# Float64 weight bits: upper word scaled as float32 on ScalarE, two VectorE operations instead of three, and a new order of all engines

## The chip, the cores and the metric

One NeuronCore of a Trainium2 chip runs the whole kernel. The metric is the time of one execution on the device in microseconds (us); less is better. TensorE does the matmuls, VectorE, ScalarE and GpSimd (DVE, ACT and POOL in the profile) work on tiles in SBUF, and SyncE (SP) issues nearly all transfers.

## The reference

Retention, a linear attention with decay, feeds a gated MLP. Batch 4, 8 heads, 768 positions, head size 64, model width 512; all inputs float32 except the MLP's weights w_in and w_out, which come as float64.

```python
for t in range(S):
    state = gamma * state + outer(k[t], v[t])
    y[t] = scale * (q[t] @ state)
x = heads side by side in y
h = gelu_tanh(x @ w_in)
u, v = h[:512], h[512:]
v_n = (v - mean(v)) / sqrt(var(v) + 1e-6) * g_ln
v_s = w_sg @ v_n (over positions) + b_sg
out = x + (u * v_s) @ w_out
```

## The kernel before, in words

The work is cut into 4 batches (b) and 2 halves of 384 positions (hf). In a half, retention handles 4 pairs of heads (p), each in 6 chunks of 64 positions: scores sc and states ds by matmul into PSUM, a mask and a scan over chunk states on VectorE, then the output po, which VectorE multiplies by a growth factor into x (line 326). For the MLP every operand is split into a rounded part and its remainder (hi and lo), and each product is three matmul passes. The products are pv and pu (the two halves of w_in), ps (positions mixed by w_sg) and py (w_out). pv, pu, ps and py share four PSUM tiles, and ds, sc and po share four others.

The order of the work is written out by hand: PROG (lines 43 to 105) is a list of words, and every engine and every DMA queue does its own part in the order of the words. A word is a step's letter, then its place. L loads a pair, P scales its keys, S, D and O are the matmuls of sc, ds and po, T is the scan, M the mask, W and K copies of the states, X makes x, H and I its hi and lo; the digits are b, hf, p, so S101 is the scores of batch 1, half 0, pair 1 (and X013 the x of batch 0, half 1, pair 3). V and U are pv and pu; G and Y are ps and py; v and u are their gelus, s the statistics of a v tile, N the reciprocal root of the variances (12 small instructions that depend on each other, lines 375 to 382), n the normalisation, a and b hi and lo of v (tile vh); e, m, h, j make the gated tile gt and its hi and lo; r and y finish the output. A last letter D, G or A names VectorE, GpSimd or ScalarE where there is a choice. ~ puts warm-up matmuls (wp) on TensorE.

Weights have words of two letters and a number. Pieces v, u and o (four each, 128 x 512 float64, 512 KB, from w_in and w_out) and s (12 of 128 x 384 float32, 192 KB, from w_sg) are loaded by l. A float64 piece is then turned into a float32 with bit operations: k (ScalarE, line 175) takes the absolute value of the upper word read as a float32, b (VectorE) does three operations on it (lines 183, 184, 187) that move the exponent and mantissa into float32's places and add the sign, r (ScalarE, line 196) rounds the lower word, a (GpSimd, line 202) adds it. h and o then make hi and lo (line 223). A pair's load (L) is one kt of 384 KB and two mw of 192 KB, all on SyncE's queue with the weights, in the order of the words.

Of the kernel before, what the change touches and what calls it, by code (L numbers as in the profile page):

```python
# [48 lines left out]
lu1 T002 H010A D003 I010G M003 W0020A U0000 W0021A bu3 V0001 P012A V0021 X011 K002 au3 V0011 C012 T003 H011A
P013A S012 W0030A I011D O002 W0031G M012 hu3A D012 ro3 K003 S013 X002 L100 C013 ou3D H002A O003 ku1 T012 I002G  # L50
D013 ru1 ls9 M013 W0120G W0121A V0012 ls5 ls11 X003 V0002 L101 bu1 H003A V0022 O012 I003D lo2 T013 au1 P100A
lo0 U0001 hs9A ls4 X012 W0131A hs0G V0023 ls1 ls6 hu1A V0013 os9D v002 V0003 ou1D ls8 v001 s002 os0G U0100
u000 ls3 v000 s001 hs5G U0010 H012A ls2 s000 P101A W0130A I012D U0020 lo1 N00 os5G ro2 U0030 ro0 ls7 n000
U0011 ko0 n001 a000 n002 U0031 bo0 a001 ko2 U0021 hs3A bo2 hs11A O013 u003 hs1A os3D D100 hs10A X013 b000G
u002 D101 H013A T100 S100 hs4A b001G hs2A S101 u001 M100 L102 ko1 K100 V0120 ko3 ao2 M101 V0110 L103 ro1 V0121
hs8A I013D a002 os1D V0111 Q hs6A os10D V0122 hs7A b002D W1001A U0101 os7D os4D P102A V0123 bo1 u010 V0112
v012 os8D V0100 W1000A s012 os2G V0113 T101 P103A V0101 ao1 v011 U0110 W1011A s011 K101 ho1A ao0 V0102 W1010A
U0120 os11D os6D V0103 bo3 U0130 v010 s010 ho0G U0121 N01 U0131 oo1G u012 U0111 u013 n011 n012 O100 u011 n010
ao3 D102 a010 X100 a011 O101 T102 H100A b010G D103 a012 ho2A S102 b012D S103 b011D L110 I100D G0020 M103 ho3G
L111 G0000 X101 C110 oo0G M102 C111 G0021 oo3D G0001 H101G G0022 P110A oo2D G0002 I101G V1020 K102 e000 W1021G  # L60
G0010 P111A m000D V1021 W1020G h000 G0011 j000D T103 r000G V1000 G0012 W1031A K103 W1030G V1001 e001 e002 O102
m001G D110 X102 m002G h001 O103 T110 D111 H102G h002 S110 W1100A j001D S111 W1101G M110 L112 G0030 M111 j002G
C113 L113 G0110 T111 I102G C112 G0031 W1110A r001D X103 r002G W1111A V1022 V1002 H103G G0032 P112G G0111 e003
I103D Y0000 m003G P113A V1023 h003 r003G V1003 v102 j003G G0112 s102 v100 s100 Y0001 G0100 y000 G0120 G0101
G0121 G0102 G0122 e010 e011 U1000 m010D m011D Y0010 r010D r011G U1001 G0130 u100 Y0020 Y0011 Y0021 y001 V1010
y002 G0131 Y0030 G0132 h010 h011 j010D Y0031 j011G e012 V1011 m012G y003 Y0110 e013 h012 r012G Y0130 j012D
Y0100 m013G V1012 h013 r013G O110 j013D D112 X110 O111 H110G T112 D113 S112 W1120A I110D S113 X111 W1121A L200
M112 H111A Y0111 I111G M113 L201 Y0131 y011 T113 Y0101 y013 W1131G Y0120 y010 W1130G V1013 Y0121 P200G v101
s101 U1010 y012 N10 U1020 P201A U1030 n102 n100 U1021 n101 a100 U1100 a101 b100D u102 b101D a102 U1031 b102D
V1120 u103 U1011 V1121 u101 V1100 V1110 V1101 V1111 O112 D200 X112 O113 H112A T200 D201 I112G S200 K200 X113  # L70
S201 W2001G M200 L202 H113A V1122 I113G M201 V1102 L203 W2000G V1123 V1103 T201 v112 V1112 v110 s112 K201
U1110 W2010A s110 W2011A U1120 P202A V1113 U1121 v111 s111 P203A U1111 u112 N11 U1130 u111 U1101 n110 n112
a110 U1131 n111 u110 b110G a111 a112 O200 u113 b111D D202 X200 b112G O201 T202 D203 H200G W2020A S202 W2021A
S203 K202 M202 L210 I200G G1020 T203 C210 L211 G1100 X201 C211 K203 W2031A M203 G1021 H201A W2030A I201D G1101
G1022 P210G G1000 G1102 P211A G1010 G1001 G1011 G1002 G1012 e100 m100D G1030 e101 h100 r100G G1130 j100D m101D
G1031 e102 h101 r101G G1131 m102D j101D h102 G1032 r102G G1132 e103 j102D Y1000 m103G e110 Y1010 m110G h103
Y1020 r103D j103G O202 r110G D210 X202 O203 H202A T210 D211 I202G S210 W2101A W2100G S211 X203 L212 M210 H203A
Y1001 C213 I203G T211 C212 L213 Y1011 M211 W2110G Y1021 y100 W2111G y101 V2020 y102 G1120 P212A V2021 V2000
V2022 V2001 P213G V2023 V2002 v202 G1121 s202 U2000 V2003 U2001 v200 s200 U2010 u200 V2010 U2011 V2011 u201
G1122 V2012 G1110 V2013 G1111 v201 s201 Y1030 N20 G1112 h110 j110G Y1031 e111 n202 U2020 e112 m111D O210 m112D  # L80
h111 n201 h112 D212 y103 j111G O211 X210 T212 H210A D213 I210G S212 e113 W2121A S213 j112D L300 W2120A M212
m113G Y1120 T213 L301 h113 Y1110 M213 W2131A W2130G Y1130 X211 j113D U2021 H211A r111D n200 Y1121 u202 I211G
P300A Y1131 a200 r112D a201 r113G y112 Y1111 a202 b200D P301A U2030 y113 b201G y111 V2120 b202G V2100 U2031
V2101 u203 V2110 V2121 V2111 Y1100 O212 D300 X212 O213 H212G T300 D301 W3001A K300 S300 I212D S301 W3000G X213
L302 M300 H213A V2122 M301 Y1101 L303 T301 V2112 I213D V2102 W3011A y110 W3010G V2113 V2123 K301 v211 V2103
P302A s211 v212 U2100 v210 s212 U2110 s210 P303A N21 U2120 U2130 n210 n211 U2111 a210 n212 a211 b210G U2131
a212 u211 U2121 b212G u213 U2101 u212 b211G G2010 u210 G2030 G2000 G2031 G2001 G2032 G2020 G2002 G2021 e200
m200G G2100 r200D h200 G2022 j200D G2101 G2011 G2102 G2012 O300 e201 e202 D302 m201G X300 O301 H300A T302
# [496 lines left out]
```

## Time and profile before

| | |
|---|---|
| median of 3 runs | 412.82 us (412.26 to 413.41) |
| profiled execution | 414.86 us, its span 413.1 us |
| busy: TensorE | 400.7 us (97%) |
| busy: VectorE, GpSimd, ScalarE | 247.1, 155.2, 146.6 us |
| chain that ended last | TensorE 78%, VectorE 9%, DMA 9% |

Read first what TensorE does by stretch of time, then, where it waits, on whom. The busy time of matmuls is modelled from their starts, so the distance from one start to the next says more than the duration of one. A duration of a VectorE instruction includes what it waited for a port while running.

### The profile page before, as it was taken

How to read it: one execution, taken by the hardware profiler on the slowest of the kernel's cores; microseconds unless marked ns; L12 is line 12 of the kernel's file. 1: busy time of each engine (PE TensorE's matmuls, PEld its weight loads, DVE VectorE, ACT ScalarE, POOL GpSimd, SP SyncE). 2: the span in 40 equal slices, each digit the busy share in tenths (PEclk: the TensorE clock that was granted, in tenths of full speed). 3: DMA queues.
4: the chain of work that ended last, by engine and by line, in shares of the span. 5: the costliest groups of instructions: out<-in, count | busy, mean ns of one | idle time of the engine just before them, and what ended most of it. 6: DMA issues, size and time to landing. Idle time of an engine off the chain costs nothing.

```text
span 413.1 us, 9386 instructions
## 1 busy us (share of the span) xinstructions
PE 400.7 (97%) x3937; PEld 366.1 (89%) x3940; DVE 247.1 (60%) x488; ACT 146.6 (35%) x266; POOL 155.2 (38%) x161
## 2 busy tenths in 40 slices
PE   8998997999999999999999899999999999999996
PEld 3657886989999998999999898899998999899996
DVE  2799899987632674672761492741746855262652
ACT  4597687623411223442121152430234312230010
POOL 3446533638721530341651154230544133302421
PEclk9999999999999999999999999999999999999999
DMA  7999785032501070514042042500243210000012
GB/s 236 289 311 251 247 299 190 6 90 66 155 19 40 21 229 1 155 27 129 2 129 82 2 141 89 152 22 2 73 141 102 72 59 21 2 0 2 0 58 96
DMA packets 18123, 41.39 MB, mean 100 GB/s; under 512 B 2464, under 2 KB 8096, under 8 KB 18080
## 3 DMA queue, kind: packets, MB, share of 16 engines
q1 hardware_dynamic: 17936, 40.51, 32.6%
q8 instruction: 31, 0.51, 0.5%
q10 hardware_dynamic: 144, 0.27, 0.2%
q14 instruction: 12, 0.10, 0.1%
HBM read 34.48 MB, written 6.29 MB: 99 GB/s over the span
## 4 chain that ended last, share of the span: by engine, by line
PE 78%; DVE 9%; DMA 9%; issue 1%; ACT 1%; SPq 0%; ACTq 0%
PE ps L424 24%; PE py L462 16%; PE pv L351 13%; PE pu L407 13%; PE po L319 5%; DMA mw<-in_qv_dram 5%; PE sc L278 4%; PE ds L270 4%; DMA raw<-in_w_v_dram 2%; DMA tab<-in_c_tab_dram 1%; DMA raw<-in_w_sg_dram 1%; DVE ws L223 1%; DVE st L365 1%; DVE wx L187 1%; DVE mw L296 1%
## 5 line engine op out<-in xcount | busy, mean ns | idle before, releaser
L424 PE MATMUL ps<-ws,vh 128*128 128x384 f32 x576 | 105.7, 336 | 0.0
L424 PEld LDWEIGHTS ps<-ws,vh 128*128 128x128 f32 x576 | 100.6, 188 | 1.6
L407 PE MATMUL pu<-xh,wu 128*128 128x384 f32 x384 | 73.0, 339 | 1.6 <-DVE gt L434 1.1
L351 PE MATMUL pv<-wv,xh 128*128 128x512 f32 x288 | 74.1, 396 | 0.0
L462 PE MATMUL py<-gh,wo 128*128 128x384 f32 x384 | 72.1, 336 | 0.0
L407 PEld LDWEIGHTS pu<-xh,wu 128*128 128x128 f32 x384 | 67.5, 188 | 3.8 <-DVE gt L434 1.4
L462 PEld LDWEIGHTS py<-gh,wo 128*128 128x128 f32 x384 | 67.0, 188 | 0.7
L351 PEld LDWEIGHTS pv<-wv,xh 128*128 128x128 f32 x288 | 53.2, 188 | 9.5
L148 ACT COPY mw<-sq 64x320 f32<-64x320 f32 (+1 forms) x44 | 36.2, 822 | 29.9 <-DVE sq L283 29.6
L434 DVE SCALAR_TENSOR_TENSOR gt<-ps,gb 128x384 f32<-128x384 f32 x32 | 19.3, 612 | 43.8 <-PE ps L424 43.7
L449 ACT CAST gh<-gt 128x384 fp32r<-128x384 f32 x32 | 16.4, 514 | 74.5 <-POOL gt L445 31.3
L296 DVE TENSOR_TENSOR mw<-sc,tab 64x384 f32<-64x384 f32 x64 | 35.5, 555 | 9.4 <-PE sc L278 7.9
L365 DVE BATCH_NORM_STATS2 st<-v 128x6 f32<-128x512 f32 x24 | 16.4, 683 | 31.4 <-ACT v L361 31.4
L473 POOL TENSOR_TENSOR o<-xh 128x384 f32<-128x384 f32 x16 | 18.0, 1125 | 40.6 <-DVE gt L445 40.3
L326 DVE TENSOR_TENSOR x<-po,tab 128x384 f32<-128x384 f32 x32 | 17.6, 549 | 25.0 <-PE po L319 20.4
L278 PE MATMUL sc<-mw,kt 64*64 64x64 f32 x768 | 27.4, 219 | 5.1 <-DVE x L326 3.6
L477 DVE TENSOR_TENSOR o<-py,o 128x384 f32<-128x384 f32 x32 | 17.4, 552 | 25.0 <-PE py L462 24.9
L278 PEld LDWEIGHTS sc<-mw,kt 64*64 64x64 f32 x768 | 24.7, 135 | 8.0 <-DVE x L326 3.9
L283 DVE TENSOR_TENSOR_SCAN sq<-step,ds 128x384 f32<-128x384 f32 x32 | 30.1, 941 | 2.3 <-PE ds L270 1.6
L319 PEld LDWEIGHTS po<-mw 128*64 128x64 f32 (+1 forms) x768 | 26.2, 137 | 5.8 <-issue 3.7
L445 POOL TENSOR_TENSOR gt<-gt,u 128x384 f32<-128x384 f32 x18 | 19.2, 1071 | 31.7 <-DVE gt L434 31.7
L319 PE MATMUL po<-mw 128*64 128x64 f32 (+1 forms) x768 | 31.0, 226 | 0.0
(61 smaller groups left out, 420.2 us busy)
## 6 DMA issues: line engine op xcount, KB each, us to landing
kt<-in_kk_dram SPq DMA_DIRECT2D x32, 384.0 KB, 5.3
mw<-in_qv_dram SPq DMA_DIRECT2D x64, 192.0 KB, 5.3
out_dram<-o SPq DMA_DIRECT2D x32, 192.0 KB, 1.8
raw<-in_w_sg_dram SPq DMA_DIRECT2D x12, 192.0 KB, 7.2
raw<-in_w_v_dram SPq DMA_DIRECT2D x4, 512.0 KB, 7.2
raw<-in_w_u_dram SPq DMA_DIRECT2D x4, 512.0 KB, 8.6
raw<-in_w_out_dram SPq DMA_DIRECT2D x4, 512.0 KB, 7.6
gb<-in_gb_dram SPq DMA_DIRECT2D x1, 386.0 KB, 4.5
```

What stands on the lines that cost most here:

```text
L148: nc.scalar.copy(out=out, in_=in_)
L278: mm(out=scs[u][o, c], lhsT=kt[i, c], rhs=mv[j][i, c], start=True, stop=True)
L283: nc.vector.tensor_tensor_scan(out=sqs[u].rearrange("p e c -> p (e c)"), data0=step_t[:, p].rearrange("p e c -> p (e c)"), data1=dss.pop(u ...
L296: nc.vector.tensor_tensor(out=mv[j][h], in0=sc[h], in1=mask_t[h, p : p + 1, :].to_broadcast([64, NCH, C]), op=ALU.mult,)
L319: mm(out=pos[u][o, c], lhsT=w[j][i, c], rhs=mv[j][i, c], start=True, stop=True)
L351: mm(out=pv[b, hf, k], lhsT=x[:, p, a, k * 128 : (k + 1) * 128], rhs=wv_t[:, w, p], start=(p == 0 and n == 0), stop=(p == NP - 1 and n == 2),)
L365: nc.vector.bn_stats(out=st, in_=vt[b, hf, k])
L407: mm(out=pu[b, hf, f], lhsT=wu_t[:, w, f, p * 128 : (p + 1) * 128], rhs=x[:, p, a], start=(n == 0), stop=(n == 11),)
L424: mm(out=ps[b, hf, d], lhsT=vh[b, t][:, v, d * 128 : (d + 1) * 128], rhs=ws_t[hf * NT + t][:, w], start=(n == 0), stop=(n == 3 * NT - 1),)
L434: nc.vector.scalar_tensor_tensor(out=t, in0=ps.pop((b, hf, d)), scalar=g_t[:, d : d + 1], in1=b_t[:, hf * HT : (hf + 1) * HT], op0=ALU.mul ...
L445: engines[e].tensor_tensor(out=t, in0=t, in1=ut.pop((b, hf, d)), op=ALU.mult)
L462: mm(out=py[b, hf, c], lhsT=wo_t[c][:, w, d * 128 : (d + 1) * 128], rhs=gh[b, hf, d][:, a], start=(d == 0 and n == 0), stop=(d == 3 and n ...
```

## The change

It does two things. The step k no longer takes the absolute value: it multiplies the upper word, read as a float32, by 2^-112, which lowers the exponent field by 112 and keeps sign and mantissa. The step b then shifts left by 3 and takes the sign from the upper word: two VectorE operations for three. And PROG is replaced as a whole; the same words stand in another order, some with another engine (twelve more of them on GpSimd), with 67 warm-up matmuls for 68. The table's rows say nothing one by one; two of each are shown. Line numbers below the edited functions fall by two.

```diff
--- before.py
+++ after.py
@@ -41,67 +41,68 @@
 
 
 PROG = """
-~40 lv0 R lv2 L000 lv3 L001 rv0 kv2 rv2 bv2 L010 kv0 bv0 P000A lu2 S000 av2 D000 M000 kv3 ~9 av0 rv3 T000 L011
-hv2A W0000A bv3 hv0A lv1 S001 P001A ov0D W0001A D001 ls10 ov2G M001 O000 lu0 av3 X000 P010A lu3 S010 H000A ~8
...
+~40 lv2 lv0 L000 lv3 L001 rv2 R kv2 kv0 lv1 bv2 rv0 lu2 bv0 lu0 av2 P000A S000 av0 hv2A D000 M000 rv3 L010 ~11
+ov2G kv3 T000 bv3 W0000A W0001A hv0G S001 P001A L011 av3 O000 M001 rv1 D001 ov0G hv3A X000 ~9 ru2 ov3D H000A
...
@@ -169,23 +170,20 @@
         nc.sync.dma_start(out=t, in_=src)
         raw[m, i] = t
 
-    def w_abs(m, i):
+    def w_scale(m, i):
+
+
         hf = raw[m, i].bitcast(F32).rearrange("p (n t) -> p n t", t=2)[:, :, 1]
         x = wx[m, i] = act.tile([128, DF], F32, tag="gh", name="wx", bufs=4)
-        nc.scalar.activation(out=x, in_=hf, func=AF.Abs)
+        nc.scalar.activation(out=x, in_=hf, func=AF.Copy, scale=2.0**-112)
 
     def w_bits(m, i):
 
-
         hi = raw[m, i].bitcast(I32).rearrange("p (n t) -> p n t", t=2)[:, :, 1]
-        x = wx[m, i]
-        xi = x.bitcast(I32)
-        nc.vector.tensor_scalar(out=x, in0=x, scalar1=2.0**-15, scalar2=None, op0=ALU.max)
-        nc.vector.tensor_scalar(
-            out=xi, in0=xi, scalar1=0x07FFFFFF, scalar2=3, op0=ALU.bitwise_and, op1=ALU.logical_shift_left
-        )
+        xi = wx[m, i].bitcast(I32)
+        nc.vector.tensor_scalar(out=xi, in0=xi, scalar1=3, scalar2=None, op0=ALU.logical_shift_left)
         nc.vector.scalar_tensor_tensor(
-            out=xi, in0=hi, scalar=-0x40000000, in1=xi, op0=ALU.bitwise_and, op1=ALU.bitwise_or
+            out=xi, in0=hi, scalar=-0x80000000, in1=xi, op0=ALU.bitwise_and, op1=ALU.bitwise_or
         )
 
     def w_round(m, i):
@@ -501,7 +499,7 @@
     def gate_constants():
         nc.sync.dma_start(out=gb_t, in_=gb)
 
-    weight_steps = {"l": w_load, "k": w_abs, "b": w_bits, "r": w_round, "a": w_sum, "h": w_hi, "o": w_lo}
+    weight_steps = {"l": w_load, "k": w_scale, "b": w_bits, "r": w_round, "a": w_sum, "h": w_hi, "o": w_lo}
     steps = {
         "L": a_load, "Z": a_load_rest, "P": a_keys, "C": a_carry_in, "D": a_states, "S": a_scores, "T": a_scan, "M": a_mask,
         "W": a_beside, "K": a_carry_out, "O": a_out, "X": a_grow, "H": a_hi, "I": a_lo,
```

VectorE's order, from the end of the first reciprocal root (word N00; line 382 before, 380 now): before, up to the mask of batch 1. wx is a float64 weight piece, v a tile of the MLP, ws a remainder of w_sg, sq the scan, mw the mask's result.

```order
L382 SCALAR_TENSOR_TENSOR lny<-lnt,lny 128x3
L387 TENSOR_SCALAR v<-v,mvar,lny 128x512 x3
L183 TENSOR_SCALAR wx<-wx 128x512
L184 TENSOR_SCALAR wx<-wx 128x512
L187 SCALAR_TENSOR_TENSOR wx<-raw,wx 128x512
L183 TENSOR_SCALAR wx<-wx 128x512
L184 TENSOR_SCALAR wx<-wx 128x512
L187 SCALAR_TENSOR_TENSOR wx<-raw,wx 128x512
L223 TENSOR_TENSOR ws<-raw,ws 128x384
L326 TENSOR_TENSOR x<-po,tab 128x384
L283 SCALAR_TENSOR_TENSOR sq<-step,ds 128x384
L296 TENSOR_TENSOR mw<-sc,tab 64x384 x4
```

The same place now, from the end of the first reciprocal root on.

```order
L380 SCALAR_TENSOR_TENSOR lny<-lnt,lny 128x3
L324 TENSOR_TENSOR x<-po,tab 128x384
L385 TENSOR_SCALAR v<-v,mvar,lny 128x512 x2
L221 TENSOR_TENSOR ws<-raw,ws 128x384
L395 TENSOR_TENSOR vh<-v,vh 128x512
L385 TENSOR_SCALAR v<-v,mvar,lny 128x512
L281 SCALAR_TENSOR_TENSOR sq<-step,ds 128x384
L294 TENSOR_TENSOR mw<-sc,tab 64x384 x4
L395 TENSOR_TENSOR vh<-v,vh 128x512
```

Two weight pieces (o0 and o2) have left the place between the normalisation and x; x (X013) now follows the root at once.

TensorE's order in batch 0, from the matmuls of half 1, pair 2 (before) to the long run of pu; 12 sc or po stand for 24 passes in the trace.

```order
L278 MATMUL sc<-mw,kt 64x64 x12
L319 MATMUL po<-mw 64x64 x12
L270 MATMUL ds<-mw,kt 64x64 x10
L278 MATMUL sc<-mw,kt 64x64 x12
L319 MATMUL po<-mw 64x64 x12
L270 MATMUL ds<-mw,kt 64x64 x10
L351 MATMUL pv<-wv,xh 128x512 x9
L319 MATMUL po<-mw 64x64 x12
L407 MATMUL pu<-xh,wu 128x384 x6
L351 MATMUL pv<-wv,xh 128x512 x9
L407 MATMUL pu<-xh,wu 128x384 x42
```

The same place now, from the po of half 0, pair 2 (O002) on.

```order
L317 MATMUL po<-mw 64x64 x12
L405 MATMUL pu<-xh,wu 128x384 x6
L276 MATMUL sc<-mw,kt 64x64 x12
L268 MATMUL ds<-mw,kt 64x64 x10
L349 MATMUL pv<-wv,xh 128x512 x9
L317 MATMUL po<-mw 64x64 x12
L276 MATMUL sc<-mw,kt 64x64 x12
L268 MATMUL ds<-mw,kt 64x64 x10
L317 MATMUL po<-mw 64x64 x12
L405 MATMUL pu<-xh,wu 128x384 x6
L349 MATMUL pv<-wv,xh 128x512 x9
L405 MATMUL pu<-xh,wu 128x384 x24
```

The last sc of batch 0 (S013, the second sc row of both) stands later: one po and nine pv that came behind it are now ahead of it. The run of pu behind the last nine pv has 24 matmuls for 42.

SyncE's queue of loads from the program's start, before: raw is a weight piece, kt and mw a pair's load.

```order
L169 DMA raw<-in_w_v_dram 128x512 x2
L238 DMA kt<-in_kk_dram 128x768
L247 DMA mw<-in_qv_dram 64x768 x2
L169 DMA raw<-in_w_v_dram 128x512
L238 DMA kt<-in_kk_dram 128x768
L247 DMA mw<-in_qv_dram 64x768 x2
L238 DMA kt<-in_kk_dram 128x768
L247 DMA mw<-in_qv_dram 64x768 x2
L169 DMA raw<-in_w_u_dram 128x512
L238 DMA kt<-in_kk_dram 128x768
```

The same queue now.

```order
L170 DMA raw<-in_w_v_dram 128x512 x2
L236 DMA kt<-in_kk_dram 128x768
L245 DMA mw<-in_qv_dram 64x768 x2
L170 DMA raw<-in_w_v_dram 128x512
L236 DMA kt<-in_kk_dram 128x768
L245 DMA mw<-in_qv_dram 64x768 x2
L170 DMA raw<-in_w_v_dram 128x512
L170 DMA raw<-in_w_u_dram 128x512 x2
L236 DMA kt<-in_kk_dram 128x768
L245 DMA mw<-in_qv_dram 64x768 x2
```

Behind the second pair's load, three more weight pieces (v1, u2, u0) stand ahead of the third pair's load (L010).

## Rows read from the trace of the kernel before

**Rows 1.** Busy time of each engine by stretch; instruction counts (x), clock, DMA share, GB/s.
```profile
core 0: us, PE busy (x) PEld busy (x) DVE busy (x) ACT busy (x) POOL busy (x), PEclk, DMA share, GB/s
8.00:33.00 25.00, 23.08 (x333) 15.18 (x335) 21.73 (x36) 18.21 (x32) 11.95 (x11) 1.00 1.04 290
33.00:53.60 20.60, 19.50 (x311) 16.48 (x308) 18.04 (x30) 15.09 (x28) 12.27 (x14) 1.00 0.91 247
53.60:86.85 33.25, 30.14 (x333) 27.34 (x331) 31.77 (x74) 21.20 (x41) 12.36 (x11) 1.00 0.41 142
87.00:409.00 322.00, 320.55 (x2950) 304.30 (x2951) 174.26 (x349) 88.95 (x163) 115.78 (x118) 1.00 0.22 68
```

**Rows 2.** TensorE's waits by what it waited for: us in total, times, longest.
```profile
PE sc L278 <- DVE x L326: 3.6, 2, 2.9
...
PE pu L407 <- DVE gt L434: 1.1, 1, 1.1
```

**Rows 3.** TensorE in order of time: start us, us, operation, count, [idle before].
```profile
19.05 0.91 PE L278 MATMUL sc<-mw,kt 64*64 64x64 f32 x24
...
20.12 1.67 PE L492 MATMUL wp<-warm 128*128 128x512 bf16 x7 [0.16 <-issue]
...
43.27 0.87 PE L278 MATMUL sc<-mw,kt 64*64 64x64 f32 x24
...
49.93 2.25 PE L351 MATMUL pv<-wv,xh 128*128 128x512 f32 x9
...
66.23 0.91 PE L278 MATMUL sc<-mw,kt 64*64 64x64 f32 x24 [2.91 <-DVE x L326]
...
87.35 1.77 PE L278 MATMUL sc<-mw,kt 64*64 64x64 f32 x48 [0.70 <-DVE x L326]
```

**Rows 4.** Chain that ended last, full stretches of matmul: start us, us, what.
```profile
267.68 8.32 PE pu L407 x48
...
343.55 0.85 PE po L319 x24
...
346.71 1.40 PE sc L278 x48
...
354.24 5.59 PE pv L351 x24
```

**Rows 5.** VectorE in order of time, 53.6 to 87 us.
```profile
53.60 0.68 DVE L365 BATCH_NORM_STATS2 st<-v 128x6 f32<-128x512 f32 x1
...
60.19 0.42 DVE L183 TENSOR_SCALAR wx<-wx 128x512 f32<-128x512 f32 x1
60.65 1.39 DVE L184 TENSOR_SCALAR wx<-wx 128x512 int32<-128x512 int32 x1
62.07 1.65 DVE L187 SCALAR_TENSOR_TENSOR wx<-raw,wx 128x512 int32<-128x512 int32 x1
63.64 0.41 DVE L183 TENSOR_SCALAR wx<-wx 128x512 f32<-128x512 f32 x1
...
86.75 0.55 DVE L326 TENSOR_TENSOR x<-po,tab 128x384 f32<-128x384 f32 x1
```

**Rows 6.** Lines 183, 184, 187: count, ns minimum/median/maximum, first and last start us.
```profile
L183 DVE TENSOR_SCALAR wx<-wx x12: 393/420/1521, 7.9 to 79.1; 128x512 f32<-128x512 f32 x12
...
L184 DVE TENSOR_SCALAR wx<-wx x12: 426/428/1394, 8.3 to 80.6; 128x512 int32<-128x512 int32 x12
...
L187 DVE SCALAR_TENSOR_TENSOR wx<-raw,wx x12: 692/693/1648, 8.8 to 81.1; 128x512 int32<-128x512 int32 x12
```

**Rows 7.** VectorE groups in 53.6 to 86.85 us (busy us, mean ns); then GpSimd by time.
```profile
L223 DVE TENSOR_TENSOR ws<-raw,ws 128x384 fp32r<-128x384 f32 x8 | 5.3, 697 | 0.0
...
L338 DVE TENSOR_TENSOR xh<-x,xh 128x384 fp32r<-128x384 f32 x2 | 1.3, 647 | 0.0
...
L397 DVE TENSOR_TENSOR vh<-v,vh 128x512 fp32r<-128x512 f32 x1 | 0.7, 677 | 0.0
...
60.14 3.02 POOL L397 TENSOR_TENSOR vh<-v,vh 128x512 fp32r<-128x512 f32 x2 [7.01 <-ACT vh L393]
```

**Rows 8.** Groups of ScalarE by line, whole span: busy us, mean ns.
```profile
L196 ACT ACTIVATE raw<-raw 128x512 int32<-128x512 uint32 x12 | 8.1, 672 | 6.7 <-DMA raw<-in_w_out_dram 3.6 <-DMA raw<-in_w_v_dram 3.0
...
L175 ACT ACTIVATE wx<-raw 128x512 f32<-128x512 f32 x12 | 7.9, 668 | 3.3 <-DMA raw<-in_w_v_dram 3.3
```

More of the change, by code (lines that the diff above doesn't have):

```diff
@@ L49 @@
[L49 to L88, printed above, removed]
@@ L104 @@
-y301 m313G h312 Y3120 j312D h313 r312D Y3130 j313G Y3100 r313G Y3111 Y3131 y311 Y3121 y313 Y3101 y312 y310
+~40 lv2 lv0 L000 lv3 L001 rv2 R kv2 kv0 lv1 bv2 rv0 lu2 bv0 lu0 av2 P000A S000 av0 hv2A D000 M000 rv3 L010 ~11
+ov2G kv3 T000 bv3 W0000A W0001A hv0G S001 P001A L011 av3 O000 M001 rv1 D001 ov0G hv3A X000 ~9 ru2 ov3D H000A
+K000 ku0 L002 I000D T001 kv1 V0010 ru0 V0000 bv1 ku2 V0020 ls9 W0011A bu0 W0010A S010 ls0 bu2 P010A O001 C010
+M010 K001 D010 av1 C011 L003 ~3 X001 T010 P011A S011 H001G hv1G D011 W0100A M011 I001G ~4 W0101A ov1G T011
@@ new lines @@
+O010 P002A S002 au0 W0111A X010 D002 ls3 M002 W0110A L012 hs0G V0001 H010A T002 au2 hu0A V0011 lu1 V0021
+W0020A L013 I010D hu2A O011 ou0D P003A os0G S003 ls7 W0021A X011 D003 lo0 H011A ou2D O002 I011D lu3 M003 K002
+U0000 C012 P012G X002 S012 T003 H002A D012 ku1 I002D ru1 M012 W0030G V0012 L100 W0031A V0002 K003 bu1 C013
+V0022 T012 au1 O003 P013A S013 W0120A X003 W0121G D013 H003A M013 hu1A I003G O012 L101 ro0 T013 ou1G ku3 U0001
+X012 ls2 ru3 ls8 V0013 H012A bu3 ls5 ko0 V0023 lo3 v001 bo0 V0003 u000 ls4 v002 U0010 s001 au3 v000 ls11
@@ new lines @@
+W0130A s002 U0020 I012G hu3A s000 lo2 U0011 W0131A ao0 N00 ls1 P101A U0021 lo1 u001 ou3G P100A Q O013 u002
+ls10 hs5A D100 hs3G X013 D101 n000 ko3 n001 S100 a000 os5D H013A S101 b000D a001 L102 n002 ro3 V0120 T100
+I013G a002 U0030 ls6 ro2 M101 b001G ko2 V0121 M100 L103 ko1 U0031 K100 ro1 os3G W1001A V0122 b002D hs10A V0110
+bo2 u003 V0123 W1000A bo3 V0111 v012 V0100 s012 ao2 P102A V0112 hs1A T101 V0101 hs9A hs11G V0113 W1010A os9D
+os1D V0102 v011 os11D U0100 W1011A s011 K101 hs4G hs2A V0103 hs6A os10D hs7A os2D U0101 v010 bo1 P103A U0110
@@ new lines @@
+u010 s010 os6G hs8A U0120 N01 os4G U0111 ao3 U0121 u011 os7D n011 O100 u012 n012 D102 n010 X100 ao1 a010 O101
+T102 a011 D103 H100A b010D S102 a012 os8D W1020A S103 b012D L110 W1021A M102 I100G G0020 L111 ho1G M103 C110
+G0000 b011G X101 C111 V1020 H101A G0001 oo1D ho2A I101D ho3A G0010 ho0G oo3D P110A V1021 oo0D G0011 oo2G G0002
+K102 T103 G0021 P111G e000 K103 G0012 W1030G G0022 m000D e001 W1031G h000 G0030 r000D j000G G0100 m001G e002
+G0031 m002D h001 V1000 r001D h002 j001G G0032 j002D V1001 e003 r002G G0101 m003D Y0000 r003D h003 j003G G0102
```

61 lines of the change are left out of this document (43 added, 18 removed).

## Prediction

> **What bounds the kernel now.** I first read the busy time of the engines by stretch [rows 1]. From 87 us on TensorE is busy 320.6 of 322 us, at a granted clock of 1.00 as in every stretch, and VectorE 174 of 322: a shorter job for VectorE can gain little there. What can be gained lies before, in three stretches. From 8 to 33 us the loads run at 290 GB/s with the DMA engines full. From 33 to 53.6 us VectorE is busy 18.0 of 20.6 us while loads still come at 247 GB/s. From 53.6 to 86.85 us VectorE is busy 31.8 of 33.25 us, and the rest are gaps of some 0.02 us between instructions that depend on each other.
>
> The list of TensorE's waits says who pays. Its longest entry is scores (sc) behind VectorE's x of line 326: 3.6 us in two waits [rows 2]. The timeline places them at S101, 66.23 us, which stood 2.91 us, and at S102, 87.35 us, which stood 0.70 us [rows 3]. Both need a PSUM tile that an x (X013, X100) has to empty, and X100 starts at 86.75 us, at the end of a queue on VectorE that runs without a hole from the first statistics at 53.60 us [rows 5]. So up to 87 us the kernel is bound first by its loads, then by the sum and order of VectorE's work.
>
> **The three operations become two.** Per 512-column piece of weights the first tensor_scalar (max, line 183) goes. Its median is 0.42 us, its longest 1.52 [rows 6]; from its start to the next one's it is some 0.02 us more, 0.44. Of the 12 pieces those before 33 us lie beside loads and give nothing by themselves; in VectorE's full stretch there were four (o0, o2, o1, o3).
> ScalarE's Abs takes 668 ns, and its Copy with a scale on the same kind of strided 512 columns 672 ns [rows 8]. I cost that edit at nothing; ScalarE, busy 21.2 of 33.25 us in that stretch [rows 1], covers it, and without cover it would be 12 x 4 ns. For a shift alone no row exists. Its bounds are 0.43 us, the median of the fused and-and-shift of the same tile (line 184), and 0.69 us, that of the piece's third operation (line 187) [rows 6]; I take 0.43, since shape, type and engine are the same. The other end costs 0.26 us a piece, 0.8 us for three.
>
> **VectorE's stretch in the new order.** From the first statistics to X100 it is 86.75 - 53.60 = 33.15 us long [rows 5]. By the listing of the new order these leave it: the piece o0 (moved ahead of the statistics), 63.64 - 60.19 = 3.45 us [rows 5]; both xh remainders, 1.3 us; four of the eight ws remainders, while three others come in, net one at 5.3 / 8 = 0.66 us [rows 7]. One vh remainder comes in, 0.68 us [rows 7]. The three pieces that stay lose their first operation: 2 x 0.44, plus 0.44 to 1.54 us for o3, which met the longest case, perhaps a wait that falls on the next instruction instead. Sum: 33.15 - 3.45 - 1.3 - 0.66 + 0.68 - (1.3 to 2.4) = 27.1 to 26.0 us; I take 26.6. X013 also moves from behind o0 and o2 to right behind the reciprocal root, so it comes before S101 wants its tile, and the 2.91 us go.
>
> **TensorE's path in the new order.** The loads are reordered: ahead of the load for S010 there are three weight pieces more (3 x 512 KB, 5.3 us at 290 GB/s), so S010, at 19.05 us before [rows 3], may come as late as 24.4 us. That is the first bound. The loads up to that of S013 are 10304 KB instead of 9920 KB (the sums follow from the queue's order and tile sizes): 384 KB more at 290 GB/s, 1.3 us. S013 started at 43.27 us [rows 3], so at latest 44.6 us if its load set it. From S010 on TensorE itself needs 18.6 us to reach S013 (five sc 3.5, five po 4.25, five ds at po's rate 3.8, six pu 1.04, 18 pv 4.2 [rows 4], seven warm-ups 1.67 [rows 3]): 43.0 us, so the load decides and I take 44.6. Then come only S013 0.7, ds 0.7, po 0.85, six pu 1.04 and nine pv 2.1 us [rows 4]: the nine pv end at 50.0 us, where before they ended at 49.93 + 2.25 = 52.18 us [rows 3].
> From there to S102 the new order has 72 pu (12.5 us), 36 pv (8.4), three po (2.55), four ds (3.4) and one double sc (1.4): 28.2 us [rows 4]. Before, it had 12 pu more (2.08 us): 30.3 us of work in 87.35 - 52.18 = 35.2 us, with 3.6 us of waits for x and 1.3 us of small ones; of these I keep 0.8, a choice between none and all. S102 by this path: 50.0 + 28.2 + 0.8 = 79.0 us.
> By VectorE: the stretch begins 1.42 us behind the nine pv, as before (53.60 - 52.18), at 51.4 us; plus 26.6 us to X100, plus the 0.6 us from X100 to S102: 78.6 us. The two paths meet, so VectorE stops being alone in setting the end, and every further microsecond would have to come from both.
> To 79.0 us I add one wait of VectorE behind GpSimd, 1.54 - 0.44 = 1.1 us, since in such a stretch they occur (below): S102 at 80.1 us, 7.25 us before the old 87.35. The 12 pu (2.08 us) are only moved behind this point and must be done in the full part: gain 5.2 us. Twelve words more on GpSimd, from ScalarE and VectorE, cost nothing while its idle time hides them (it was busy 12.4 of 33.25 us [rows 1]); without that cover each is some 1 us on a chain.
>
> **Behind 87 us.** All engines are in a new order, with the same matmuls. The one visible wait of TensorE there is a pu group for VectorE's gt, 1.1 us [rows 2]: gt stood behind the chain of the reciprocal root. In the new order that pu takes a tile that ScalarE empties, so it should go; I set against it new waits of the same size. Sum: -5.2 us. The profiled execution took 414.86 us (span 413.1), so 409.7 by it; the three timed runs have their median 2.04 us below it, so I forecast 412.82 - 5.2 = **407.6 us**, its own range being 406 to 409.5.
>
> **Rivals.**
> - *Every wait goes* (0.13): the load of S013 was early before, TensorE sets it at 43.0 us, no wait behind GpSimd falls on the path, and the 1.1 us at gt goes as well. S102 then comes 1.6 us earlier and without the added 1.1, at 77.4 us: 87.35 - 77.4 - 2.08 + 1.1 = 9.0 us, 403.8 us. For it: S013 followed its predecessor without a wait. Against: so tight an order leaves a wait somewhere.
> - *The loads eat it* (0.17): with 1.5 MB ahead of S010, the nine pv end at 52.2 us as before. Then S102 is at 52.2 + 28.2 + 0.8 + 1.1 = 82.3 us, gain 3.0, 409.8 us. For it: DMA is full up to 33 us [rows 1]. Against: by the sum above the load of S013 is only 1.3 us later, with less work behind it.
> - *VectorE gets nothing back* (0.12): the waits behind GpSimd grow. In the piece o0 the second operation took 1.39 us and the third 1.65 [rows 5], where the medians are 0.43 and 0.69 [rows 6], while GpSimd worked at two vh from 60.14 to 63.16 us [rows 7]. With the moved work four to six more of 1 us each would give 411.6 to 413.5 us. The Trainium skill (SBUF — State Buffer, section "SBUF: two separate sides") states that VectorE and GpSimd share one port pair under an exclusive lock and that the loser blocks for the other's whole instruction. The trace agrees in the durations just named; by that rule a removed operation's wait only passes to the next one, and work moved to GpSimd is paid on VectorE.
> - *Slower* (0.10): the wait for gt repeats. Behind each of the other seven reciprocal-root chains an instruction that empties a PSUM tile can be queued, and TensorE, with four such tiles, stands 1.1 us each time [rows 2]. It decides from six such waits on: 6 x 1.1 exceeds 5.2 + 1.2. All seven would give 412.82 - 5.2 + 7.7 = 415.3 us. For it: the whole later order is new. Against: only one of eight did so before.
>
> **How the numbers follow.** The forecast itself has 0.48. About 0.3%, 1.2 us, is what a measurement here can tell from no change (the three runs spread over 1.15 us). Faster than 411.6 us are the forecast, the late loads and the case without waits: 0.78. Same: 0.12. Slower: 0.10. The range is 404.0 to 412.6 us: it leaves out about half of the first rival, the upper end of the third and the slower one, 0.2 in all.
>
> **What would show it.** Right, if S101 follows S100 without a wait, the first long ps stretch starts at about 82 us instead of 89.05, VectorE's stretch from the first statistics to X100 is 26 to 27 us, the shift takes 0.43 us, and TensorE is full behind. Wrong in the first step, if the nine pv before the long pu stretch end at 52 us or later; wrong in the second, if VectorE's undisturbed durations stay but single ones reach 1.3 us and more; wrong altogether, if TensorE's waits behind 87 us add up to more than 5 us.

## The result, and the profile after

The changed kernel takes 412.04 us (median of 20 executions, 410.15 to 413.73); the kernel before, on the same chips, 414.93 us (20 executions, 412.26 to 417.93). The ratio is 0.9933, 95% interval 0.9913 to 0.9953: 0.7%, or 2.9 us by the medians, faster. The forecast was 5.2 us, 1.3% faster. The profiled executions agree: a span of 410.1 us against 413.1. (The forecast of 407.6 us also started from three executions whose median lay 2.1 us lower than that of the twenty; the comparison below is of gains.)

Busy time by stretch in the changed kernel; the columns are those of [rows 1].

```profile
8.00:33.00 25.00, 22.65 (x336) 15.25 (x340) 17.86 (x28) 15.85 (x27) 13.50 (x14) 1.00 1.04 288
33.00:53.60 20.60, 20.60 (x316) 17.69 (x311) 18.85 (x28) 16.40 (x31) 13.20 (x15) 1.00 0.96 260
53.60:86.85 33.25, 29.88 (x369) 26.94 (x369) 31.98 (x71) 22.32 (x42) 18.03 (x17) 1.00 0.48 152
87.00:409.00 322.00, 319.71 (x2906) 303.59 (x2905) 177.40 (x345) 83.09 (x155) 121.19 (x122) 1.00 0.22 68
```

From 33 to 53.6 us TensorE now has no hole. In the third stretch it still stands for 3.4 us, VectorE is as full as before, and GpSimd works 18.0 us where it had 12.4 [rows 1].

TensorE's waits in the changed kernel, as in [rows 2]: the one for gt is gone, and the total for x is nearly what it was.

```profile
PE sc L276 <- DVE x L324: 3.4, 2, 3.0
PE wp L490 <- DVE warm L481: 1.2, 1, 1.2
PE sc L276 <- DMA mw<-in_qv_dram: 0.8, 2, 0.5
```

TensorE in order of time, as in [rows 3]: S010, S013, the last nine pv, S101 and S102.

```profile
23.82 0.29 PE L276 MATMUL sc<-mw,kt 64*64 64x64 f32 x2 [0.49 <-DMA mw<-in_qv_dram]
...
45.26 0.91 PE L276 MATMUL sc<-mw,kt 64*64 64x64 f32 x24
...
48.69 2.25 PE L349 MATMUL pv<-wv,xh 128*128 128x512 f32 x9
...
58.74 0.92 PE L276 MATMUL sc<-mw,kt 64*64 64x64 f32 x24 [0.32 <-DVE x L324]
...
79.29 0.92 PE L268 MATMUL ds<-mw,kt 64*64 64x64 f32 x24
83.25 1.77 PE L276 MATMUL sc<-mw,kt 64*64 64x64 f32 x48 [3.04 <-DVE x L324]
84.96 2.37 PE L422 MATMUL ps<-ws,vh 128*128 128x384 f32 x12
```

S101's 2.91 us have shrunk to 0.32, but S102, which had stood 0.70 us [rows 3], now stands 3.04. Both wait for an x to empty a tile: the wait has not gone, it has moved 25 us on.

VectorE before S102, as in [rows 5].

```profile
50.38 1.33 DVE L184 TENSOR_SCALAR wx<-wx 128x512 int32<-128x512 int32 x1 [0.39 <-ACT wx L178]
51.75 1.39 DVE L185 SCALAR_TENSOR_TENSOR wx<-raw,wx 128x512 int32<-128x512 int32 x1
53.06 0.68 DVE L363 BATCH_NORM_STATS2 st<-v 128x6 f32<-128x512 f32 x1
...
58.13 0.56 DVE L324 TENSOR_TENSOR x<-po,tab 128x384 f32<-128x384 f32 x1
...
67.03 1.69 DVE L185 SCALAR_TENSOR_TENSOR wx<-raw,wx 128x512 int32<-128x512 int32 x1
...
73.84 1.25 DVE L184 TENSOR_SCALAR wx<-wx 128x512 int32<-128x512 int32 x1
75.12 1.39 DVE L185 SCALAR_TENSOR_TENSOR wx<-raw,wx 128x512 int32<-128x512 int32 x1
...
77.73 1.20 DVE L375 TENSOR_SCALAR lny<-lna 128x3 int32<-128x3 int32 x1
...
82.65 0.55 DVE L324 TENSOR_TENSOR x<-po,tab 128x384 f32<-128x384 f32 x1
```

GpSimd in the same stretch, in order of time.

```profile
73.47 2.49 POOL L221 TENSOR_TENSOR ws<-raw,ws 128x384 fp32r<-128x384 f32 x2 [1.69 <-ACT ws L149]
75.92 2.99 POOL L200 TENSOR_TENSOR wx<-wx,raw 128x512 int32<-128x512 int32 x2
```

Lines 184 and 375 by themselves, as in [rows 6].

```profile
L184 DVE TENSOR_SCALAR wx<-wx x12: 393/423/1335, 7.0 to 73.8; 128x512 int32<-128x512 int32 x12
...
L375 DVE TENSOR_SCALAR lny<-lna x8: 168/170/1203, 55.8 to 354.2; 128x3 int32<-128x3 int32 x8
```

The shift costs 0.42 us, as forecast. But line 375, three elements a lane, took 1.20 us for its 0.17: it ended at 78.93 us, and GpSimd's pair of wx at 75.92 + 2.99 = 78.91 us. That is how a wait behind GpSimd reads: a longer duration, not a gap. The first x (X013) comes at 58.13 us, the one for S102 (X100) at 82.65: 29.59 us from the first statistics, where I had 26.6.

### The profile page after: what moved, and what is told of

It reads as the page before. It is cut to its first block, busy times and chain, and to the rows that moved or that the text cites. A ratio compares the mean times of both kernels' runs of the same rounds, so it can differ in the third digit from the quotient of the medians.

```text
span 410.1 us, 9396 instructions
## 1 busy us (share of the span) xinstructions
PE 399.8 (97%) x3935; PEld 366.2 (89%) x3939; DVE 247.5 (60%) x473; ACT 140.4 (34%) x257; POOL 168.9 (41%) x173
## 4 chain that ended last, share of the span: by engine, by line
PE 79%; DMA 11%; DVE 7%; issue 1%; ACT 1%; SPq 0%
PE ps L422 25%; PE py L460 17%; PE pu L405 13%; PE pv L349 12%; DMA mw<-in_qv_dram 6%; PE po L317 5%; PE sc L276 4%; PE ds L268 4%; DMA kt<-in_kk_dram 3%; DMA raw<-in_w_u_dram 2%; DVE wx L185 1%; DVE st L363 1%; DVE v L385 1%; DVE wx L184 1%; DVE ws L221 1%
## 5 line engine op out<-in xcount | busy, mean ns | idle before, releaser
L422 PE MATMUL ps<-ws,vh 128*128 128x384 f32 x576 | 107.4, 336 | 0.0
L349 PE MATMUL pv<-wv,xh 128*128 128x512 f32 x288 | 76.9, 398 | 0.0
L405 PE MATMUL pu<-xh,wu 128*128 128x384 f32 x384 | 74.7, 339 | 0.0
L460 PE MATMUL py<-gh,wo 128*128 128x384 f32 x384 | 73.6, 336 | 0.0
L349 PEld LDWEIGHTS pv<-wv,xh 128*128 128x128 f32 x288 | 52.9, 188 | 8.9 <-DVE o L475 0.4
L149 ACT COPY mw<-sq 64x320 f32<-64x320 f32 (+1 forms) x40 | 32.8, 820 | 24.2 <-DVE sq L281 23.8
L443 POOL TENSOR_TENSOR gt<-gt,u 128x384 f32<-128x384 f32 x15 | 15.8, 1056 | 54.4 <-DVE gt L432 54.1
L336 POOL TENSOR_TENSOR xh<-x,xh 128x384 fp32r<-128x384 f32 x20 | 22.6, 1129 | 37.4 <-ACT xh L149 31.6
L415 ACT ACTIVATE u<-pu 128x384 f32<-128x384 f32 x32 | 15.5, 488 | 61.1 <-PE pu L405 60.8
L451 POOL TENSOR_TENSOR gh<-gt,gh 128x384 fp32r<-128x384 f32 x19 | 21.4, 1131 | 29.8 <-ACT gh L447 29.6
L475 DVE TENSOR_TENSOR o<-py,o 128x384 f32<-128x384 f32 x32 | 17.4, 551 | 24.2 <-PE py L460 24.2
```

What stands on the lines that cost most here:

```text
L149: nc.scalar.copy(out=out, in_=in_)
L336: engines[e].tensor_tensor(out=t[:, p, 1], in0=xs.pop((b, hf, p)), in1=t[:, p, 0].bitcast(F32), op=ALU.subtract)
L349: mm(out=pv[b, hf, k], lhsT=x[:, p, a, k * 128 : (k + 1) * 128], rhs=wv_t[:, w, p], start=(p == 0 and n == 0), stop=(p == NP - 1 and n == 2),)
L405: mm(out=pu[b, hf, f], lhsT=wu_t[:, w, f, p * 128 : (p + 1) * 128], rhs=x[:, p, a], start=(n == 0), stop=(n == 11),)
L422: mm(out=ps[b, hf, d], lhsT=vh[b, t][:, v, d * 128 : (d + 1) * 128], rhs=ws_t[hf * NT + t][:, w], start=(n == 0), stop=(n == 3 * NT - 1),)
L451: engines[e].tensor_tensor(out=g[:, 1], in0=gts.pop((b, hf, d)), in1=g[:, 0].bitcast(F32), op=ALU.subtract)
```

## The experiments

Two readings of each trace serve throughout. **Stretch** is the time on VectorE from the first statistics to X100. **Waits** is what its instructions there took beyond the lower quartile of their own line, operation and shape in the whole trace, where that is over 0.1 us; **rest** is stretch less waits. All 70 waits counted in the table began while a GpSimd instruction was running. The last column is the span less the start of S102.

| kernel | S102 at | stretch | waits (count) | rest | GpSimd busy in it | behind S102 |
|---|---|---|---|---|---|---|
| before | 87.35 | 33.14 | 4.86 (7) | 28.29 | 12.6 | 325.7 |
| edit alone | 83.73 | 31.44 | 5.00 (7) | 26.44 | 12.9 | 326.0 |
| order alone | 85.66 | 31.30 | 5.42 (10) | 25.88 | 15.9 | 329.2 |
| changed | 83.25 | 29.59 | 5.10 (9) | 24.48 | 16.5 | 326.9 |
| changed, second profile | 81.91 | 30.38 | 5.93 (10) | 24.45 | 17.4 | 326.9 |
| words off GpSimd | 83.95 | 30.15 | 4.46 (6) | 25.70 | 11.5 | 328.8 |
| GpSimd's words repeated | 86.16 | 31.20 | 6.59 (11) | 24.61 | 21.5 | 329.3 |
| ps ahead of S102 | 82.28 | 30.37 | 5.94 (10) | 24.43 | 17.5 | 325.2 |

**1. The edit alone**, in the order of before.

```diff
-        nc.scalar.activation(out=x, in_=hf, func=AF.Abs)
+        nc.scalar.activation(out=x, in_=hf, func=AF.Copy, scale=2.0**-112)
...
-        nc.vector.tensor_scalar(out=x, in0=x, scalar1=2.0**-15, scalar2=None, op0=ALU.max)
...
```

> The order of the kernel before, with the scaled upper word and two VectorE operations. Theory A (a wait behind GpSimd does not vanish with an operation, it passes to the next one): the four weight pieces in VectorE's full stretch lose 4 x 0.44 us, S102 starts 1.8 us earlier (about 85.5 us), S101's wait shrinks from 2.9 to about 2.0 us, the time falls by 1.8 us, ratio 0.9957. Rival B (the waits go with the operation): the pieces o0, o2, o1, o3 lose 0.42 + 0.41 + 0.41 + 1.51 us of line 183 and the waits of o0's other two operations shrink too, S102 at 84.5 us or earlier, ratio 0.993 or less, which would be all of the change's gain. Rival C (the edit gives nothing, the order all): S102 at 87 us, ratio 0.999 to 1.0.

0.9955 (0.9923 to 0.9986), span 409.7. The rest shrank by 1.85 us, which is four pieces at 0.44 and a little; the waits stayed (4.86 to 5.00). S101 waited 1.4 us for its x and S102 not at all. S102's 83.73 us are below the 84.5 of rival B, but not for its reason: the stretch began 1.93 us earlier (51.67 us for 53.60), in a part of the kernel that differs that much between executions, and itself lost 1.70 us.

**2. The order alone**, with the three old operations.

```diff
-        nc.vector.tensor_scalar(out=xi, in0=xi, scalar1=3, scalar2=None, op0=ALU.logical_shift_left)
+        nc.vector.tensor_scalar(out=x, in0=x, scalar1=2.0**-15, scalar2=None, op0=ALU.max)
...
```

> The new order with the old three operations. Theory A: the pieces o0, o2, o3, o1 (and to a part u3) stand on VectorE's way to X100, each 0.44 us longer, so S102 comes 1.3 to 2.2 us later than in the changed kernel (84.6 to 85.5 us against 83.25), and the time is 1 to 1.7 us below the kernel before, ratio 0.996 to 0.998. Rival C (the order alone carries the gain): ratio 0.993, S102 at 83.3 us. Rival B (the edit alone carries it): ratio 1.0.

1.0048 (1.0022 to 1.0075): slower, which no theory had. The trace has S102 waiting 4.76 us, and a clock that falls in the wait. TensorE at S102, then the columns of [rows 1] for 82 to 92 us:

```profile
85.66 2.83 PE L279 MATMUL sc<-mw,kt 64*64 64x64 f32 x48 [4.76 <-DVE x L327]
88.41 3.64 PE L425 MATMUL ps<-ws,vh 128*128 128x384 f32 x12
```

```profile
82.00:84.00 2.00, 0.00 (x0) 0.00 (x0) 1.79 (x9) 0.00 (x0) 0.00 (x0) 1.00 0.00 0
84.00:86.00 2.00, 0.34 (x6) 0.35 (x8) 2.00 (x5) 0.83 (x2) 0.00 (x0) 0.60 0.00 0
86.00:88.00 2.00, 2.00 (x44) 2.00 (x42) 2.00 (x4) 1.99 (x5) 1.15 (x1) 0.50 0.00 0
88.00:90.00 2.00, 2.00 (x15) 1.88 (x12) 1.93 (x5) 0.88 (x2) 2.00 (x3) 0.50 0.85 261
```

S102 comes 1.7 us earlier than before, but the 12 pu (2.08 us) are now behind it: no gain. What lies behind S102 is 329.2 us where the changed kernel, in the same order, has 326.9: with the granted clock at 0.50 (1.2 GHz) the double sc took 2.83 us for 1.77 and the twelve ps 3.64 for 2.37. These 2.3 us of clock are more than the span's loss (414.9 us for 413.1): at full clock this execution would have been about even with the kernel before. So the order alone is not the gain: 1.0048 and 0.9955 would make 1.000, the two together give 0.9933. With the edit the wait at S102 is 3.0 us instead of 4.8, and in the profiled execution the clock stayed at 1.00.

**3. Words taken off GpSimd**: in the changed kernel three casts of w_sg go to ScalarE and three remainders to VectorE.

```diff
-hs3G os3G hs11G hs4G os6G os4G
+hs3A os3D hs11A hs4A os6D os4D
```

> The changed kernel, with the casts of s3, s11, s4 moved from GpSimd to ScalarE and the remainders of s3, s6, s4 from GpSimd to VectorE, as far as they lie in VectorE's stretch up to X100. Theory A (GpSimd's work is paid on VectorE): VectorE has 3 x 0.47 us more of its own, but its operations in the stretch that took 1.2 to 1.7 us instead of 0.42 to 0.69 (piece o1, and the reciprocal root) fall to two or three; the stretch from the statistics to X100 stays within 0.7 us of 29.6 us, ratio to before 0.992 to 0.995. Rival D (only VectorE's own sum counts, its long operations have another cause): the long operations stay as many (six), the stretch grows by 1.4 us to 31.0, ratio 0.997.

0.9978 (0.9952 to 1.0004). VectorE's own work rose by 1.2 us (rest 24.48 to 25.70) and its stretch by 0.56 only, since the waits fell from 5.10 in nine instructions to 4.46 in six. The direction is theory A's, its time was missed: the nine pv, which lie ahead of every word that was moved, ended at 52.59 us (50.94 in the changed kernel's profile), and the clock was 0.50 in 26 to 28 and in 84 to 86 us.

**4. GpSimd's words repeated**: four of its words in the changed kernel's stretch are done two or three times, 5.0 us more work for GpSimd and none for any other engine.

```diff
+AGAIN = {("b", 0, 0, 1): 2, ("o", "s", 3): 2, ("h", "s", 11): 2, ("h", "s", 4): 3}
...
-        copy(e, w_parts(m, i)[0], wx[m, i])
+        for _ in range(AGAIN.get(("h", m, i), 1)):
+            copy(e, w_parts(m, i)[0], wx[m, i])
```

> The changed kernel, with four of GpSimd's instructions in VectorE's stretch done again in place where GpSimd was idle behind them (the remainder of v of half 0, tile 1, and of s3 twice, the cast of s11 twice, of s4 three times): some 4.5 us more on GpSimd, nothing more on VectorE. Theory A (GpSimd's work is paid on VectorE): VectorE's stretch from the statistics to X100 grows from 29.6 us by 1.5 to 4 us, S102 by as much, the time by 1 to 4 us, ratio to before 0.996 to 1.003. Rival D (GpSimd's idle time hides it): stretch 29.6 +/- 0.3 us, ratio 0.993.

0.9985 (0.9962 to 1.0008). The rest is 24.61 us, as in the changed kernel; the waits rose from 5.10 to 6.59. S102 came at 86.16, 2.9 us later: 1.3 us because the stretch began later (54.36 us), ahead of every repeated word, and 1.6 us by the stretch itself. TensorE's list of waits there begins:

```profile
PE sc L280 <- DVE x L328: 4.7, 1, 4.7
```

Where VectorE's additional waits lie, with GpSimd beside them:

```profile
66.83 1.23 DVE L185 TENSOR_SCALAR wx<-wx 128x512 int32<-128x512 int32 x1
68.10 1.40 DVE L186 SCALAR_TENSOR_TENSOR wx<-raw,wx 128x512 int32<-128x512 int32 x1
65.88 3.07 POOL L225 TENSOR_TENSOR ws<-raw,ws 128x384 fp32r<-128x384 f32 x2
```

In the changed kernel GpSimd was idle at this weight piece, and the two took 0.41 and 0.69 us; here the repeated remainders of v and s3 keep GpSimd busy, and they wait 0.82 and 0.71 us. This shows the mechanism: nothing but GpSimd's work changed, and VectorE waited 1.5 us more for 5.0. But all of it is one meeting at one piece; the other repeats met nothing that waits, so 0.3 us for a microsecond is an average and no price.

The table says the same in the other direction. One wait in it, 0.83 us in the first instruction of the first root, comes and goes with the execution: it is in the second profile, in "words off GpSimd" and in "ps ahead of S102", and not in the other rows of the new order. Without it the three rows of the changed kernel's work have 5.1 us each, and "words off GpSimd" has 3.6: 1.5 us less for 5.0 us less of GpSimd work.

**5. X100 moved early**: O100, X100, D102 and T102 go ahead of the last statistics and the root in the changed kernel (the tile xh is then taken at X's cast instead of at X).

```diff
-u010 s010 os6G hs8A U0120 N01 os4G U0111 ao3 U0121 u011 os7D n011 O100 u012 n012 D102 n010 X100 ao1 a010 O101
-T102 a011 D103 H100A
+u010 O100 X100 D102 T102 s010 os6G hs8A U0120 N01 os4G U0111 ao3 U0121 u011 os7D n011 u012 n012 n010 ao1 a010 O101
+a011 D103 H100A
```

> The changed kernel, with po, x, ds and scan (O100, X100, D102, T102) moved ahead of the second reciprocal root (N01) in the order; the buffer of x's hi and lo is taken at the cast and not at x. Same work. Theory A with VectorE's queue as the only cause of S102's wait: S102 starts at about 80.3 us without a wait instead of 83.25, the root and normalisation end 1.3 us later, so the second ps group waits about 1 us; net 1.5 to 2.5 us less than the changed kernel, ratio to before 0.987 to 0.990. Rival E (the normalised v, not x, sets the pace behind S102): the wait only moves to the ps groups, the time stays within 0.5 us of the changed kernel, ratio 0.992 to 0.994.

0.9887 (0.9837 to 0.9937), and S102 at 79.52 us without a wait. But what lies behind it grew to 329.7 us: pv of batch 1 now waited for the cast and the remainder of X100 (0.4 us each) and for the cast of X101 (1.3). The kernel once more:

> The kernel with x early (e4) once more beside e9: ratio to before 0.987 to 0.991, mean clock 0.998 or more in most executions, since TensorE no longer stands ahead of S102.

0.9934 (0.9908 to 0.9959): no gain over the changed kernel can be claimed. Moving the cast and X101 forward as well made it worse:

```diff
-os7D n011
+os7D H100A n011
...
-W1020A S103 b012D L110 W1021A M102 I100G
+W1020A S103 b012D I100G X101 H101A L110 W1021A M102
```

> The kernel with x early (e4), with the cast of that x (H100) ahead of the normalisation's casts on ScalarE, and its remainder (I100), the next x (X101) and its cast (H101) ahead of the mask M102 in the order: the waits of the two pv groups behind S102 for xh (1.7 us in two on ScalarE, 0.4 us on GpSimd in e4). Theory A (VectorE's queue up to S102 was the place; what is left are these waits): they go, 1 to 2 us less than e4, ratio to before 0.983 to 0.987. Rival E (the normalised v sets the pace there): the wait moves to the ps groups that need the new vh, the time stays within 0.5 us of e4, ratio 0.988 to 0.990.

1.0032 (1.0009 to 1.0054). The remainder of X101 on VectorE now stood behind the masks and an o remainder, and TensorE stopped twice:

```profile
86.62 0.73 PE L349 MATMUL pv<-wv,xh 128*128 128x512 f32 x2 [1.68 <-ACT xh L149]
90.54 0.80 PE L349 MATMUL pv<-wv,xh 128*128 128x512 f32 x1 [3.18 <-DVE xh L336]
```

**6. The wait filled with useless matmuls**: 14 of pu's shape, whose result nothing reads, ahead of S102; first in the changed kernel, then in the order alone.

```diff
-D103 H100A b010D S102
+D103 H100A b010D ! S102
...
+    def fill():
+        t = psm.tile([128, HT], F32, tag="m", name="fill")
+        for _ in range(14):
+            mm(out=t, lhsT=wu_t[:, 0, 0, :128], rhs=xn[0, 1][:, 0, 0], start=True, stop=True)
```

> The changed kernel, with 14 matmuls of no use (2.4 us) put on TensorE between the last ds and S102, where it stood 3.0 us idle. Theory F (behind that idle stretch the granted clock falls in most executions, as it shows 0.53 from 84 to 90 us in the run with the new order alone): S102 starts where it did (83.3 us), the mean clock is 0.998 or more in most executions instead of 0.991 to 0.996, and the time falls by 0.8 to 1.5 us, ratio to before 0.990 to 0.992. Rival G (the lower clock has another place or cause): clocks as before, time equal or up to 0.5 us longer, ratio 0.993 to 0.995.

0.9930 (0.9902 to 0.9958). The mean clock was 0.998 or more in 9 of 11 executions, where the changed kernel, measured beside it, had that in 2 of 12; yet the median is the changed kernel's. The interval reaches down to the 0.990 that theory F forecast, so a small gain is not excluded. That the clock is not what took the rest of the gain, executions at full clock (a mean of 0.998 or more) tell better: beside this run, on the same chip, the two of the changed kernel took 410.6 and 410.8 us, the five of the kernel before a median of 413.8, a gain of 3.1 us where all of them give 2.7.

> The new order with the old three operations, and the same 14 matmuls ahead of S102, where that kernel stood 4.8 us. Theory F: the clock no longer falls to 0.53 from 84 to 90 us, the time falls by 2 to 3 us against the new order alone (417.2 to about 414.5 us), ratio to before 0.998 to 1.001, so that the order by itself is worth nothing. Rival H (order alone is slower by its own waits): time stays at 416.5 us or more, ratio 1.004 or more.

1.0042 (1.0016 to 1.0068), the same as without. The fill did not end the wait here (2.13 us remained, and the clock was 0.50 in 88 to 90 us), so the medians do not tell how much of the order's loss is clock. Two of its ten executions ran at a mean clock of 1.000 and took 414.5 and 415.0 us, against a median of 416.3 and against 413.8 for the kernel before at full clock: this speaks for the larger part, from two executions only.

**7. The changed kernel again**, with a second profile.

> The changed kernel once more, beside the others on one chip: ratio to before 0.991 to 0.995. Theory F: in an execution with a mean clock of 0.996 or less, the clock is below 0.9 in a stretch behind S102's wait (84 to 90 us). Rival G: the lower clock lies elsewhere, as in 20 to 30 us.

0.9936 (0.9913 to 0.9959). The second profile has VectorE's stretch start at 50.92 us instead of 53.06 and last 30.38 instead of 29.59: the first instruction of the first root took 1.00 us for 0.17, beside a remainder on GpSimd that in the first profile had all but ended by then (waits 5.93, and 5.10 without this one). S102's wait is 3.05 us here and 3.04 there. This execution has a mean clock of 0.999, so where the clock falls in the others it could not show.

**8. Work that is wanted anyway goes into the wait**: TensorE's order alone, in the changed kernel. Eighteen ps of batch 0 go ahead of S102, the later groups move up.

```diff
-b010D S102 a012 os8D W1020A S103 b012D L110 W1021A M102 I100G G0020 L111 ho1G M103 C110
-G0000 b011G X101 C111 V1020 H101A G0001 oo1D ho2A I101D ho3A G0010 ho0G oo3D P110A V1021 oo0D G0011 oo2G G0002
-K102 T103 G0021 P111G e000
+b010D G0020 G0000 G0010 S102 a012 os8D W1020A S103 b012D L110 W1021A M102 I100G L111 ho1G M103 C110
+G0001 b011G X101 C111 G0011 V1020 H101A oo1D ho2A I101D ho3A G0021 ho0G oo3D P110A G0002 V1021 oo0D oo2G
+K102 T103 P111G e000
```

> The changed kernel with one edit in TensorE's order alone: 18 ps matmuls of batch 0 (three groups of six, on v tiles and w_sg pieces that were ready by about 76 us) go ahead of S102, and the later groups move up so that each pv of batch 1 stays at about its old time; the four other queues are the same word for word. Theory A (the wait of 3.0 us at S102 is time in which TensorE had other work ready; VectorE's end at X100 is not on the path of that work): the 18 ps take 3.1 us in the wait, S102 stays at 83.3 us with a wait under 0.5 us, and the kernel ends up to 3 us earlier: ratio to the kernel before 0.986 to 0.988. Rival R (VectorE's end sets the end anyway, because the pv, masks and scans of batch 1 hang on X100): the wait comes back at the pv of batch 1 or at later groups, as where X100 was moved early: ratio 0.992 to 0.995, with 2 to 3 us of new waits between 85 and 100 us. Rival M (the ps met a v tile or a w_sg piece that is late): the ps themselves wait before 83 us, ratio between the two.

0.9884 (0.985 to 0.9918), span 407.5 us. TensorE from 78 us on:

```profile
78.10 0.92 PE L268 MATMUL ds<-mw,kt 64*64 64x64 f32 x24
78.95 3.40 PE L422 MATMUL ps<-ws,vh 128*128 128x384 f32 x18
82.28 1.61 PE L276 MATMUL sc<-mw,kt 64*64 64x64 f32 x48
...
92.64 3.79 PE L422 MATMUL ps<-ws,vh 128*128 128x384 f32 x18 [0.86 <-DVE gt L432]
```

S102 follows without a wait, and behind it lie 325.2 us, 1.7 less than in the changed kernel: the 18 ps (3.1 us), less a new wait of 0.86 for a tile that gt empties and some 0.5 that I cannot place. Again:

> The same kernel once more (18 ps of batch 0 ahead of S102), since of two runs of the kernel with X100 moved early the first stood at 0.9887 and the second at 0.9934. If the gain over the changed kernel is real (the wait at S102 filled with work that has to be done anyway, TensorE's clock full), the ratio comes out at 0.986 to 0.990 again, S102 without a wait and a clock of 0.995 and more in most executions. If it was the draw of the executions, it comes out at 0.992 to 0.995, like the changed kernel.

0.9907 (0.9886 to 0.9927), S102 without a wait. Both runs lie below both of the changed kernel (0.9933, 0.9936), by some 0.4% on average, though each interval still touches theirs. On the average of its two runs it is the fastest version tried, though not beyond doubt ahead of X100 moved early (0.9887 and 0.9934).

## Why the prediction was right in direction and wrong in size

- **The shift and ScalarE's scale**: right. The shift's median is 0.42 us (0.43 taken); line 178, the scale, takes 665 ns on average where Abs took 668 [rows 8].
- **The loads**: the times came out within 1 us, the reason did not. S013 came at 45.26 us (44.6 forecast) and the nine pv ended at 50.94 (50.0); in the second profile at 44.27 and 49.95. But S013 followed the po ahead of it without a wait, so its load did not set it: TensorE needed 21.4 us from S010 (23.82 us) to S013, where I had 18.6 (my terms add up to 18.5). That a bound by the load lay near is luck. The rival in which the loads eat the gain (nine pv at 52.2 us) is not what the two profiles of the changed kernel show, and that its gain of 3.0 us is near the measured one is chance. But the ten profiles whose words are the same up to there, those of the experiments taken in, have the nine pv end at 48.9 to 52.9 us, two of them behind 52.2, so this point differs by more from one execution to the next than the 2.2 us that I forecast there.
- **TensorE's path behind the nine pv**: right. It was done with all that comes ahead of S102 at 79.29 + 0.92 = 80.2 us, 29.3 us behind the nine pv, where I had 28.2 + 0.8.
- **S101**: right, 0.32 us left of 2.91.
- **VectorE's stretch**: the step that failed. I had 26.6 us; it is 29.59 (30.38 in the second profile). The undisturbed work came out by 28.29 - 24.48 = 3.8 us, against 4.2 in my sum (o0's three operations 1.6, xh 1.3, ws net 0.66, three first operations 1.3, less the vh 0.7). But I also took out the waits that I saw on the removed instructions: about 1.9 us in o0 and half of the 1.1 on o3's first operation. Those 2.4 us were not the instructions' own. Every kernel of the table keeps 4.5 to 6.6 us of waits in the stretch, and the one wait of 1.1 us that I put back on the path was too little. This is the second sign of being wrong that I had named: the undisturbed durations stay, and single ones reach 1.3 us and more (1.39 and 1.69 above). With the later start of the stretch (53.06 for 51.4 us, o0's two long instructions at 50.38 and 51.75 us) VectorE reached S102 4.65 us after my 78.6.
- **S102**: hence 83.25 us for 80.1. TensorE, ready at 80.2, stood 3.04 us.
- **Behind S102**: slightly better than my nothing. The 12 pu moved there cost 2.08 us, and 326.9 - 325.7 = 1.2 us were added; the wait for gt (1.1 us) went, and no new one came.
- **Sum**: (87.35 - 83.25) - 1.2 = 2.9 us, the spans' 3.0 and the medians' 2.9.

So what happened is the forecast with a part of the third rival: the waits behind GpSimd did not go with the words. Twelve more words on GpSimd, which I cost at nothing under its idle time, are not free either: GpSimd's work in the stretch rose from 12.6 to 16.5 us, and in experiments 3 and 4 some 5 us of such work less or more moved VectorE's waits by 1.5 us. The Trainium skill (SBUF — State Buffer, section "SBUF: two separate sides"), which the rival named, states a lock that one of the two engines holds for its whole instruction while the other waits. The trace agrees: line 375 took 1.20 us for 0.17 and ended within 0.03 us of GpSimd's instruction. My price was for more waits of 1 us each; what the runs show is a total that hardly falls when words are taken out of VectorE.

The edit and the order are also not two gains that add. The edit alone gave 0.45%, the order alone lost 0.48%, together they gained 0.67%: the order gathers TensorE's waits into one ahead of S102, and with the edit that one is 1.7 us shorter (3.04 us for 4.76), with no fall of the clock behind it in the two profiles.

## What to carry to other kernels

Sum a stretch of VectorE as undisturbed durations plus one total for its waits behind GpSimd, and do not strike out the long case with the instruction that shows it: which of VectorE's instructions meet GpSimd's sets the total. Where a changed order moves a wait instead of removing it, look for work that is wanted anyway, is ready, and can stand in that place; here a move of 18 matmuls on one engine was worth about as much as the edit (0.4%, in two runs whose intervals touch those without it). Measure an edit and the new order apart, since one of them can lose.
